# Keys and queries of a hash attention split on 128 rows for two heads and laid out by transfers, with the vector engine's constants first

## The chip, the cores and the metric

The kernel runs on one core of one Trainium2 chip. The metric is the device time of one execution in microseconds. Five engines work in order, each from its own queue: PE (TensorE, matrix products), DVE (VectorE), ACT (ScalarE), POOL (GpSimd) and SP (SyncE), which in this kernel issues every transfer.

## What is computed

An attention over hashed keys, followed by two feed-forward layers. The shapes: 2 batches, 8 heads, 768 positions, 64 numbers per head; 1536 tokens of width 512, inner width 2048.

```python
q_bits = (einsum('bhsd,dk->bhsk', q, proj) > 0)
k_bits = (einsum('bhsd,dk->bhsk', k, proj) > 0)
mask = q_bucket[:, :, :, None] == k_bucket[:, :, None, :]
scores = where(mask, scale * q @ k.T, -1e9)
attn = softmax(scores)
x = attn @ v                          # then heads side by side: 1536 x 512
x = relu(x @ w_in) ** 2 @ w_out
h = x @ moe2_w_in
out = (max(h, 0) + alpha * min(h, 0)) @ moe2_w_out
```

Six projections give each position one of 64 buckets; a query sees only the keys of its own bucket.

## The kernel before

**Stages.** The tokens are cut into four chunks of 384 queries (c = 0 to 3; chunks 0 and 1 are the first batch, 2 and 3 the second). In a chunk the 8 heads go as four pairs (j = 0 to 3), so there are 16 pairs. The attention of chunk 0 runs alone. Then the first layer of chunk c runs with the attention of chunk c + 1 spread over its steps by `Background`. After chunk 3's attention the rest is feed-forward alone.

**Precision.** A product in float32 is made of two rounded halves (high = x rounded to fp32r, low = x - high). For a score tile of head h the 128 contraction rows hold 64 rows of data and 64 more: `k1[r, h]` is the key's high half and `k1[o, h]` its low half, where `rows(h)` gives `r`, the 64 rows of the head, and `o`, the other 64. `q1` holds the query's high half on both. `k2[r, h]` repeats the key's high half and meets the query's low half `q2[r, h]`. `k2[o, h]` holds, per hash pattern, the mask of the keys (-2**100 where the pattern differs) and `q2[o, h]` the query's one-hot. So `scores` is two matrix products for each half of the keys: L317 (q1, k1) and L318 (q2, k2).

**Preparing a pair.** `load_pair` loads the keys `kr` and the queries `qn` as 128 rows (two heads below each other), and the queries a second time as `qr`, both heads side by side and the rows twice. `hash_bits` projects (L228) and compares (L232); `matches` turns signs into counts by products with the constant `code` (L244). In even chunks the keys are prepared: `k_split` (high half L254 on ACT, low half L256 on POOL, transfers L259 and L260 to the other tile or the other rows) and `k_ids` (L272). In every chunk the queries are: `q_split` (L279, L282) and `q_ids` (L291). Only pair (0, 0) makes its key halves without transfers (L262, L263).

**Order.** `attention` writes the steps of a chunk: the preparing steps of pair j + 1 stand one by one between the six score tiles of pair j, so in even chunks `q_ids` of the next pair is the last step before its first score tile; in odd chunks, which have two preparing steps, it comes four tiles earlier. The first pair of a chunk is prepared right ahead of its scores. A score tile is reduced on DVE (L321), exponentiated on ACT (L324), turned in two groups of three blocks on PE (L338), written to `pt` by ACT or DVE (L342, L344), and summed with the values (`av`, L354). The scheduler then places the instructions on the engines by its own forecast of times, so the order in a queue is not that of the text. Weights arrive as the bits of float64: `load_bits` (L459), `to_f32` (ACT L469, DVE L471, L472, L474), and store (L483); `fetch` loads converted weights again (L521). `we` and `wsg` have one buffer each.

```python
for u in range(2 * NTB):
    h, t = divmod(u, NTB)
    steps.append(lambda pr=pr, h=h, t=t: pr.scores(h, t))
    late.append((pr, h, t))
    if nxt and u > 0:
        steps.append(nxt.pop(0))
...
    if len(late) > lag:
        tail()
```

**Constants.** `constants` makes `code`, `pop` and `off`: five `iota` on POOL, then 20 short instructions on DVE (L150 to L168).

## Time and profile before

| | |
|---|---|
| runs | 858.56, 860.59, 863.87 us; median 860.59 |
| profiled execution | 862.17 us, of which span 860.2 us |
| busy in the span | PE 804.5 us (94%), DVE 515.6 (60%), ACT 487.4 (57%), POOL 385.7 (45%) |
| granted TensorE clock, mean | 0.987 |
| transfers | 118.66 MB, mean 138 GB/s |

The span runs from the first to the last instruction; 1.97 us of the profiled time lie around it. Matrix products overlap, so a busy PE is not PE at its peak: stages are to be compared by the products they hold and by the idle time that other engines' waits name.

### The profile page before, as it was taken

How to read it: one execution, taken by the hardware profiler on the slowest of the kernel's cores; microseconds unless marked ns; L12 is line 12 of the kernel's file. 1: busy time of each engine (PE TensorE's matmuls, PEld its weight loads, DVE VectorE, ACT ScalarE, POOL GpSimd, SP SyncE). 2: the span in 40 equal slices, each digit the busy share in tenths (PEclk: the TensorE clock that was granted, in tenths of full speed). 3: DMA queues.
4: the chain of work that ended last, by engine and by line, in shares of the span. 5: the costliest groups of instructions: out<-in, count | busy, mean ns of one | idle time of the engine just before them, and what ended most of it. 6: DMA issues, size and time to landing. Idle time of an engine off the chain costs nothing.

```text
span 860.2 us, 12647 instructions
## 1 busy us (share of the span) xinstructions
PE 804.5 (94%) x4384; PEld 652.2 (76%) x4384; DVE 515.6 (60%) x834; ACT 487.4 (57%) x941; POOL 385.7 (45%) x329
## 2 busy tenths in 40 slices
PE   4989899999888989999999999999999999999997
PEld 2656578776666666676867789989998998998995
DVE  5599798988577778787864431215444444444442
ACT  4768688776564655575755556654434444444341
POOL 3121133323746574562333345555555555555553
PEclk9999999999999999999999999999999999999999
DMA  6575666766666656767542388800001011001000
GB/s 193 141 229 183 196 224 228 248 213 220 181 204 206 203 182 198 213 218 222 163 142 67 88 302 299 288 1 37 3 34 38 1 38 37 1 0 37 1 1 37
DMA packets 54575, 118.66 MB, mean 138 GB/s; under 512 B 6928, under 2 KB 15344, under 8 KB 54512
## 3 DMA queue, kind: packets, MB, share of 16 engines
q1 hardware_dynamic: 54512, 117.87, 42.8%
q8 instruction: 34, 0.56, 0.3%
q14 instruction: 29, 0.24, 0.1%
HBM read 89.22 MB, written 23.12 MB: 131 GB/s over the span
## 4 chain that ended last, share of the span: by engine, by line
PE 55%; DVE 10%; DMA 6%; ACT 4%; issue 4%; POOL 2%; SPq 0%; POOLq 0%; DVEq 0%; ACTq 0%
PE acc L575 8%; PE acc L571 7%; PE acc L572 7%; PE m L545 4%; PE m L543 4%; PE m L544 4%; PE m L354 4%; PE h L543 4%; DMA w<-we 4%; PE h L544 4%; PE h L545 3%; DVE low L321 2%; PE m L338 1%; PE s L317 1%; DVE we L474 1%
## 5 line engine op out<-in xcount | busy, mean ns | idle before, releaser
L561 POOL TENSOR_TENSOR gl<-g,gh 128x384 fp32r<-128x384 f32 x128 | 136.5, 1066 | 244.8 <-ACT gh L560 123.0
L571 PE MATMUL acc<-wh,gh 128*128 128x512 f32 x384 | 160.0, 417 | 0.0
L496 POOL TENSOR_TENSOR wl<-wf,wh 128x512 fp32r<-128x512 f32 x80 | 109.4, 1370 | 112.4 <-ACT wh L495 99.9
L572 PE MATMUL acc<-wl,gh 128*128 128x512 f32 x384 | 152.6, 397 | 0.0
L495 ACT ACTIVATE wh<-w 128x512 fp32r<-128x512 f32 x128 | 80.5, 629 | 81.0 <-PE m L544 45.7
L575 PE MATMUL acc<-wh,gl 128*128 128x512 f32 x384 | 115.4, 399 | 1.8 <-POOL gl L561 1.8
L495 ACT ACTIVATE wh<-wf 128x512 fp32r<-128x512 f32 x128 | 80.4, 629 | 58.1 <-PE h L544 22.9
L543 PE MATMUL h<-xh,wh 128*128 128x384 f32 x296 | 106.4, 359 | 1.4 <-DVE pt L344 0.8
L544 PE MATMUL h<-xl,wh 128*128 128x384 f32 x296 | 100.6, 340 | 0.6 <-POOL xl L383 0.6
L545 PE MATMUL h<-xh,wl 128*128 128x384 f32 x296 | 100.8, 341 | 0.0
L321 DVE TENSOR_REDUCE low<-s 128x1 f32<-128x768 f32 x84 | 79.8, 950 | 24.9 <-PE s L318 24.3
L324 ACT ACTIVATE sm<-s,low 128x768 f32<-128x768 f32 x84 | 75.5, 899 | 30.0 <-DVE low L321 29.7
L338 PE MATMUL m<-ident,sm 128*128 128x128 f32 x525 | 84.9, 279 | 3.9 <-DVE pt L344 1.4
L575 PEld LDWEIGHTS acc<-wh,gl 128*128 128x128 f32 x384 | 72.0, 189 | 21.5 <-POOL gl L561 4.3
L496 POOL TENSOR_TENSOR wl<-w,wh 128x512 fp32r<-128x512 f32 x64 | 82.9, 1295 | 6.0 <-ACT wh L495 6.0
L571 PEld LDWEIGHTS acc<-wh,gh 128*128 128x128 f32 x384 | 72.4, 189 | 14.5 <-issue 5.0
L338 PEld LDWEIGHTS m<-ident,sm 128*128 128x128 f32 x525 | 65.9, 143 | 19.5 <-DVE pt L344 3.2
L572 PEld LDWEIGHTS acc<-wl,gh 128*128 128x128 f32 x384 | 72.8, 189 | 9.8 <-issue 1.8
L560 ACT ACTIVATE gh<-g 128x384 fp32r<-128x384 f32 x64 | 33.5, 524 | 81.5 <-DVE g L559 81.5
L317 PE MATMUL s<-k,q 128*128 128x384 f32 x168 | 64.4, 383 | 16.0 <-ACT sm L324 13.5
L558 DVE TENSOR_SCALAR r<-m,alpha_sb 128x384 f32<-128x384 f32 x43 | 26.6, 618 | 87.2 <-PE m L545 86.9
L545 PE MATMUL m<-xh,wl 128*128 128x384 f32 x216 | 73.0, 338 | 0.5 <-DVE wl L496 0.5
(107 smaller groups left out, 1536.8 us busy)
## 6 DMA issues: line engine op xcount, KB each, us to landing
wf<-w SPq DMA_DIRECT2D x96, 256.0 KB, 2.8
wbits<-in_w_in_dram SPq DMA_DIRECT2D x32, 512.0 KB, 4.1
wbits<-in_w_out_dram SPq DMA_DIRECT2D x32, 512.0 KB, 3.8
w<-wf SPq DMA_DIRECT2D x32, 256.0 KB, 3.3
w<-we SPq DMA_DIRECT2D x32, 256.0 KB, 2.1
w<-w SPq DMA_DIRECT2D x32, 256.0 KB, 4.5
qr<-in_qT_dram SPq DMA_DIRECT2D x32, 192.0 KB, 3.9
kr<-in_kT_dram SPq DMA_DIRECT2D x8, 384.0 KB
```

Of the source, the lines that this page charges most:

```text
L321: nc.vector.tensor_reduce(low, ps[:, 0:2, 0:HALF], AX.XY, ALU.max, negate=True)
L324: nc.scalar.activation(sm.rearrange("p (a n) -> p a n", a=2), ps[:, 0:2, 0:HALF], AF.Exp, bias=low, accum_out=self.sums[:, i:i + 1],)
L338: nc.tensor.transpose(ps[:, i * P:(i + 1) * P], pp[:, b * P:(b + 1) * P], ident)
L495: nc.scalar.activation(hi, w, AF.Copy)
L496: engine.tensor_tensor(lo, w, f32(hi), ALU.subtract)
L543: nc.tensor.matmul(hp, wih[:, ks], xh[:, kk, :], start=first, stop=False)
L544: nc.tensor.matmul(hp, wih[:, ks], xl[:, kk, :], start=False, stop=False)
L545: nc.tensor.matmul(hp, wil[:, ks], xh[:, kk, :], start=False, stop=last)
L561: nc.gpsimd.tensor_tensor(gl, g, f32(gh), ALU.subtract)
L571: nc.tensor.matmul(acc[:, t, :], gh[:, blocks[t]], woh, start=first, stop=False)
L572: nc.tensor.matmul(acc[:, t, :], gh[:, blocks[t]], wol, start=False, stop=False)
L575: nc.tensor.matmul(acc[:, t, :], gl[:, blocks[t]], woh, start=False, stop=last)
```

## The change

Three edits, and one that goes with them.

1. The 20 DVE instructions of `constants` and the comparisons L232 of pair (0, 0) are marked so that their written order is kept on the engine.
2. For all pairs but (0, 0) the halves are made on all 128 rows, both heads in one instruction, into tiles of their own (`kh`, `kn`, `qh`, `ql`, `qy`), and transfers put them into `k1`, `k2`, `q1`, `q2`. The low half of the keys moves from POOL to DVE. An even pair's keys take six transfers for the halves and two for the mask, where there were four; a pair's queries take four transfers from tile to tile, where there were two loads of `qr`.
3. `qr` is loaded for pair (0, 0) alone.
4. For room, `pt` has two buffers where it had three.

```diff
--- before.py
+++ after.py
@@ -90,7 +90,6 @@
     weight_pools(weights, 0)
     p1 = pool("p1", 1, att)
     p2 = pool("p2", 2, att)
-    p3 = pool("p3", 3, att)
     p4 = pool("p4", 4, att)
     sm3 = pool("sm3", 3, att)
 
@@ -134,6 +133,7 @@
 
         i32 = mybir.dt.int32
         with tc.tile_pool(name="once", bufs=1) as once:
+            first = tc.keep_in_program_order
             cols = once.tile([P, D], i32, name="cols")
             row = once.tile([P, 1], i32, name="row")
             bit = once.tile([P, 1], i32, name="bit")
@@ -147,25 +147,25 @@
             nc.gpsimd.iota(nb[:, 0, :], [[0, NB]], base=0, channel_multiplier=1)
             nc.gpsimd.iota(nb[:, 1, :], [[1, NB]], base=0, channel_multiplier=0)
 
-            nc.vector.tensor_copy(of, part)
+            first(nc.vector.tensor_copy(of, part))
             above = once.tile([P, 2 * NG], F32, name="above")
-            nc.vector.tensor_scalar(above, of, 0.0, None, ALU.is_ge)
...
-            nc.vector.tensor_scalar(sign, cols, 2.0, -1.0, ALU.mult, ALU.add)
+            first(nc.vector.tensor_scalar(above, of, 0.0, None, ALU.is_ge))
...
+            first(nc.vector.tensor_scalar(sign, cols, 2.0, -1.0, ALU.mult, ALU.add))
             for g in range(NG):
                 for h in range(2):
-                    nc.vector.tensor_scalar(
+                    first(nc.vector.tensor_scalar(
                         code[:, g, (1 - h) * D:(2 - h) * D], sign, of[:, 2 * g + h:2 * g + h + 1], None, ALU.mult
-                    )
-            nc.vector.tensor_tensor(nb[:, 0, :], nb[:, 0, :], nb[:, 1, :], ALU.logical_shift_right)
-            nc.vector.tensor_scalar(nb[:, 0, :], nb[:, 0, :], 1, None, ALU.bitwise_and)
+                    ))
+            first(nc.vector.tensor_tensor(nb[:, 0, :], nb[:, 0, :], nb[:, 1, :], ALU.logical_shift_right))
+            first(nc.vector.tensor_scalar(nb[:, 0, :], nb[:, 0, :], 1, None, ALU.bitwise_and))
             ones = once.tile([P, NB], F32, name="ones")
-            nc.vector.tensor_copy(ones, nb[:, 0, :])
...
+            first(nc.vector.tensor_reduce(pop, ones, AX.X, ALU.add))
+            first(nc.vector.tensor_scalar(off, pop, -1.0, 1.0, ALU.mult, ALU.add))
 
 
     xT = {}
@@ -186,11 +186,13 @@
                 )
         qn = p2.tile([P, T], F32, tag="qn", name="qn")
         nc.sync.dma_start(out=qn, in_=qT[b, h0:h0 + 2, :, s0:s0 + T].rearrange("h d s -> (h d) s"))
-        qr = p1.tile([P, 2, T], F32, tag="qr", name="qr")
-        for r in range(2):
-            nc.sync.dma_start(
-                out=qr[r * D:(r + 1) * D], in_=qT[b, h0:h0 + 2, :, s0:s0 + T].rearrange("h d s -> d h s")
-            )
+        qr = None
+        if c == 0 and j == 0:
+            qr = p1.tile([P, 2, T], F32, tag="kh", name="qr")
+            for r in range(2):
+                nc.sync.dma_start(
+                    out=qr[r * D:(r + 1) * D], in_=qT[b, h0:h0 + 2, :, s0:s0 + T].rearrange("h d s -> d h s")
+                )
         if c % 2 == 0:
             vr = p4.tile([P, NKB, 2 * D], F32, tag="vr", name="vr")
             nc.sync.dma_start(out=vr, in_=v[b, j])
@@ -208,6 +210,7 @@
         def __init__(self, c, j):
             self.c, self.j = c, j
             self.b = c // 2
+            self.first = c == 0 and j == 0
             self.p = {}
             self.pt = {}
 
@@ -229,7 +232,9 @@
                     ps[g * GR:(g + 1) * GR, 0:w], proj_sb.rearrange("p h n -> p (h n)"), x[:, g * w:(g + 1) * w],
                     start=True, stop=True,
                 )
-            nc.vector.tensor_scalar(bits, ps[:, 0:w], 0.0, None, ALU.is_gt)
+            ins = nc.vector.tensor_scalar(bits, ps[:, 0:w], 0.0, None, ALU.is_gt)
+            if self.first:
+                tc.keep_in_program_order(ins)
             return bits
 
         def matches(self, bits, n):
@@ -248,47 +253,75 @@
             self.k1 = p4.tile([P, 2, S], F32R, tag="k1", name="k1")
             self.k2 = p4.tile([P, 2, S], F32R, tag="k2", name="k2")
             keys[self.b, self.j][1:3] = [self.k1, self.k2]
-            shift = self.c > 0 or self.j > 0
+            if self.first:
+                for h in range(2):
+                    r, o = self.rows(h)
+                    nc.scalar.activation(self.k1[r, h], self.kr[r], AF.Copy)
+                    nc.vector.tensor_tensor(self.k1[o, h], self.kr[r], f32(self.k1[r, h]), ALU.subtract)
+                    nc.gpsimd.tensor_copy(self.k2[r, h], f32(self.k1[r, h]))
+                return
+            kh = p1.tile([P, S], F32R, tag="kh", name="kh")
+            nc.scalar.activation(kh, self.kr, AF.Copy)
+            nc.vector.tensor_tensor(self.kr.bitcast(F32R), self.kr, f32(kh), ALU.subtract)
             for h in range(2):
                 r, o = self.rows(h)
-                nc.scalar.activation(self.k1[r, h], self.kr[r], AF.Copy)
-                if shift:
-                    nc.gpsimd.tensor_tensor(
-                        self.kr[r].bitcast(F32R), self.kr[r], f32(self.k1[r, h]), ALU.subtract
-                    )
-                    nc.sync.dma_start(out=f32(self.k2[r, h]), in_=f32(self.k1[r, h]))
-                    nc.sync.dma_start(out=f32(self.k1[o, h]), in_=self.kr[r])
-                else:
-                    nc.vector.tensor_tensor(self.k1[o, h], self.kr[r], f32(self.k1[r, h]), ALU.subtract)
-                    nc.gpsimd.tensor_copy(self.k2[r, h], f32(self.k1[r, h]))
+                nc.sync.dma_start(out=f32(self.k1[r, h]), in_=f32(kh[r]))
+                nc.sync.dma_start(out=f32(self.k2[r, h]), in_=f32(kh[r]))
+                nc.sync.dma_start(out=f32(self.k1[o, h]), in_=self.kr[r])
 
         def k_bits(self):
             self.bits = self.hash_bits(self.kr, S)
 
         def k_ids(self):
             y = self.matches(self.bits, S)
+            if self.first:
+                for h in range(2):
+                    r, o = self.rows(h)
+                    nc.vector.tensor_scalar(
+                        self.k2[o, h].rearrange("p (a n) -> p a n", n=T), y[o], pop[o], NEG,
+                        ALU.not_equal, ALU.mult,
+                    )
+                return
+            kn = p1.tile([P, S], F32R, tag="kn", name="kn")
+            nc.vector.tensor_scalar(
+                kn.rearrange("p (a n) -> p a n", n=T), y, pop, NEG, ALU.not_equal, ALU.mult
+            )
             for h in range(2):
                 r, o = self.rows(h)
-                nc.vector.tensor_scalar(
-                    self.k2[o, h].rearrange("p (a n) -> p a n", n=T), y[o], pop[o], NEG, ALU.not_equal, ALU.mult
-                )
+                nc.sync.dma_start(out=f32(self.k2[o, h]), in_=f32(kn[o]))
 
         def q_split(self):
             self.q1 = p2.tile([P, 2, T], F32R, tag="q1", name="q1")
             self.q2 = p2.tile([P, 2, T], F32R, tag="q2", name="q2")
-            nc.scalar.activation(self.q1, self.qr, AF.Copy, scale=scale)
+            if self.first:
+                nc.scalar.activation(self.q1, self.qr, AF.Copy, scale=scale)
+            if self.first:
+                for h in range(2):
+                    r, o = self.rows(h)
+                    nc.vector.scalar_tensor_tensor(
+                        self.q2[r, h], self.qr[r, h], scale, f32(self.q1[r, h]), ALU.mult, ALU.subtract
+                    )
+            self.bits = self.hash_bits(self.qn, T)
+
+        def q_ids(self):
+            y = self.matches(self.bits, T)
+            if self.first:
+                for h in range(2):
+                    r, o = self.rows(h)
+                    nc.scalar.activation(self.q2[o, h], y[o, 0, :], AF.Relu, bias=off[o])
+                return
+            qh = p1.tile([P, T], F32R, tag="qh", name="qh")
+            qy = p1.tile([P, T], F32R, tag="qy", name="qy")
+            ql = p1.tile([P, T], F32R, tag="ql", name="ql")
+            nc.scalar.activation(qy, y[:, 0, :], AF.Relu, bias=off)
+            nc.scalar.activation(qh, self.qn, AF.Copy, scale=scale)
+            nc.vector.scalar_tensor_tensor(ql, self.qn, scale, f32(qh), ALU.mult, ALU.subtract)
             for h in range(2):
                 r, o = self.rows(h)
-                nc.vector.scalar_tensor_tensor(
-                    self.q2[r, h], self.qr[r, h], scale, f32(self.q1[r, h]), ALU.mult, ALU.subtract
-                )
-            self.bits = self.hash_bits(self.qn, T)
-
-        def q_ids(self):
-            y = self.matches(self.bits, T)
-            for h in range(2):
-                r, o = self.rows(h)
-                nc.scalar.activation(self.q2[o, h], y[o, 0, :], AF.Relu, bias=off[o])
+                nc.sync.dma_start(out=f32(self.q1[r, h]), in_=f32(qh[r]))
+                nc.sync.dma_start(out=f32(self.q1[o, h]), in_=f32(qh[r]))
+                nc.sync.dma_start(out=f32(self.q2[r, h]), in_=f32(ql[r]))
+                nc.sync.dma_start(out=f32(self.q2[o, h]), in_=f32(qy[o]))
 
         def prepare(self):
 
@@ -329,7 +362,7 @@
 
         def p_t(self, h, t, a):
             if t == 0 and a == 0:
-                self.pt[h] = p3.tile([P, NTB, NKB, P], F32, tag="pt", name="pt")
+                self.pt[h] = p2.tile([P, NTB, NKB, P], F32, tag="pt", name="pt")
             pp = self.p[h, t]
             ps = m_tile()
             n = NKB // 2
```

## Rows read from the trace of the kernel before

**Rows 1.** Busy time by stage: attention of chunk 0, 1 and 2.

```profile
core 0: us, PE busy (x) PEld busy (x) DVE busy (x) ACT busy (x) POOL busy (x), PEclk, DMA share, GB/s
17.20:89.20 72.00, 62.52 (x378) 44.41 (x378) 58.30 (x94) 54.37 (x113) 13.54 (x10) 0.95 0.60 182
89.20:218.00 128.80, 124.35 (x729) 92.50 (x729) 111.39 (x182) 96.60 (x196) 39.62 (x32) 0.99 0.69 223
218.00:352.00 134.00, 117.09 (x663) 89.62 (x662) 96.20 (x135) 78.49 (x155) 82.60 (x65) 0.96 0.64 197
```

**Rows 2.** Timeline of the start: start, duration, engine, line; idle before it in brackets.

```profile
5.39 2.45 DVE L262 TENSOR_TENSOR k<-kr,k 64x768 fp32r<-64x768 f32 x2
7.88 0.15 DVE L155 TENSOR_SCALAR bit<-row 128x1 int32<-128x1 int32 x1
...
9.37 0.56 DVE L282 SCALAR_TENSOR_TENSOR q<-qr,q 64x384 fp32r<-64x384 f32 x1
9.96 1.39 DVE L160 TENSOR_SCALAR code<-sign,of 128x64 bf16<-128x64 f32 x8
...
13.24 2.05 DVE L272 TENSOR_SCALAR k<-s,pop 64x768 fp32r<-64x768 f32 x2 [1.84 <-PE s L244]
...
15.22 0.24 DVE L232 TENSOR_SCALAR bits<-m 128x96 bf16<-128x96 f32 x1
...
16.48 1.18 ACT L291 ACTIVATE q<-h,off 64x384 fp32r<-64x384 f32 x2 [5.59 <-PE h L244]
...
17.20 0.66 PE L318 MATMUL acc<-k,q 128*128 128x384 f32 x1 [0.76 <-ACT q L291]
```

**Rows 3.** Timeline of two stretches in chunk 2's attention in which PE stands still.

```profile
233.57 0.69 PE L317 MATMUL s<-k,q 128*128 128x384 f32 x1 [3.70 <-ACT sm L324]
...
266.64 3.93 SPq L260 DMA_DIRECT2D k<-kr  x2
...
268.10 1.96 POOL L256 TENSOR_TENSOR kr<-kr,k 64x768 fp32r<-64x768 f32 x1
270.66 0.54 SPq L483 DMA_DIRECT2D w<-we  x1
273.89 0.66 ACT L469 ACTIVATE we<-wbits 128x512 f32<-128x512 f32 x1 [3.55 <-DMA w<-we]
275.90 0.49 PE L244 MATMUL s<-bits,code 128*128 128x192 bf16 x4 [3.37 <-ACT sm L324]
```

**Rows 4.** Busy time and granted clock around these two stretches (columns as in 1).

```profile
228.00:240.00 12.00, 8.30 (x35) 6.33 (x34) 2.56 (x4) 6.29 (x13) 5.28 (x5) 0.72 0.82 246
266.00:282.00 16.00, 12.63 (x73) 10.93 (x73) 11.52 (x15) 7.45 (x15) 11.21 (x10) 0.89 0.61 188
```

**Rows 5.** Groups by line and shape: count, then busy us and mean ns.

```profile
L256 POOL TENSOR_TENSOR kr<-kr,k 64x768 fp32r<-64x768 f32 x14 | 26.1, 1861 | 35.8 <-PE m L228 35.3
...
L279 ACT ACTIVATE q<-qr 128x768 fp32r<-128x768 f32 x16 | 13.4, 840 | 2.4 <-DMA qr<-in_qT_dram 1.8 <-PE acc L317 0.5
...
L382 ACT ACTIVATE xh<-x 128x384 fp32r<-128x384 f32 x16 | 8.3, 520 | 6.3 <-DVE x L381 6.2
```

**Rows 6.** Transfers: issue time at SP (min/median/max ns); size and us to landing.

```profile
L259 SPq DMA_DIRECT2D k<-k x14: 467/490/1142, 11.4 to 244.1; - x14
...
k<-k SPq DMA_DIRECT2D x14, 192.0 KB, 3.9
...
wf<-w SPq DMA_DIRECT2D x96, 256.0 KB, 2.8
```

**Rows 7.** Timeline of PE and ACT where a next pair's scores begin.

```profile
38.26 4.09 PE L354 MATMUL h<-pt,vr 128*64 128x384 f32 x24
...
98.37 0.44 PE L318 MATMUL s<-k,q 128*128 128x384 f32 x1 [0.36 <-ACT q L291]
...
283.79 1.17 ACT L291 ACTIVATE q<-m,off 64x384 fp32r<-64x384 f32 x2
287.70 0.34 PE L318 MATMUL s<-k,q 128*128 128x384 f32 x1
```

More of the change, by code (lines that the diff above doesn't have):

```diff
@@ L148, in constants @@
             nc.gpsimd.iota(nb[:, 1, :], [[1, NB]], base=0, channel_multiplier=0)
-            nc.vector.tensor_copy(of, part)
+            first(nc.vector.tensor_copy(of, part))
             above = once.tile([P, 2 * NG], F32, name="above")
-            nc.vector.tensor_scalar(above, of, 0.0, None, ALU.is_ge)
-            nc.vector.tensor_scalar(of, of, float(GR // 2), None, ALU.is_lt)
-            nc.vector.tensor_tensor(of, of, above, ALU.mult)
-            nc.vector.tensor_scalar(bit, row, GR // 2 - 1, None, ALU.bitwise_and)
@@ L156, in constants @@
-            nc.vector.tensor_scalar(cols, cols, bit, 1, ALU.logical_shift_right, ALU.bitwise_and)
-            nc.vector.tensor_scalar(sign, cols, 2.0, -1.0, ALU.mult, ALU.add)
+            first(nc.vector.tensor_scalar(above, of, 0.0, None, ALU.is_ge))
+            first(nc.vector.tensor_scalar(of, of, float(GR // 2), None, ALU.is_lt))
+            first(nc.vector.tensor_tensor(of, of, above, ALU.mult))
+            first(nc.vector.tensor_scalar(bit, row, GR // 2 - 1, None, ALU.bitwise_and))
+            first(nc.vector.tensor_scalar(cols, cols, bit, 1, ALU.logical_shift_right, ALU.bitwise_and))
@@ L165, in constants @@
+            first(nc.vector.tensor_tensor(nb[:, 0, :], nb[:, 0, :], nb[:, 1, :], ALU.logical_shift_right))
+            first(nc.vector.tensor_scalar(nb[:, 0, :], nb[:, 0, :], 1, None, ALU.bitwise_and))
             ones = once.tile([P, NB], F32, name="ones")
-            nc.vector.tensor_copy(ones, nb[:, 0, :])
-            nc.vector.tensor_reduce(pop, ones, AX.X, ALU.add)
-            nc.vector.tensor_scalar(off, pop, -1.0, 1.0, ALU.mult, ALU.add)
+            first(nc.vector.tensor_copy(ones, nb[:, 0, :]))
```

## Prediction

> **What bounds the kernel now.** I read three views in this order. First the busy time by stage [rows 1]: the stages that the change touches are the start, the attention of chunk 0 (17 to 89 us) and the attentions of chunks 1 to 3 beside the first layer; behind the last attention nothing of it is left. In these stages no engine is full by itself: in chunk 1's attention DVE is busy 111.39 of 128.8 us (86%) and ACT 96.60, in chunk 2's PE drops to 117.09 of 134 us and POOL rises to 82.60. Five queues work in order and wait for one another there, so time is lost where a queue's head waits, not where an engine is slow.
>
> Second, the timeline of the start [rows 2]. The first score tile can't be finished before L318 at 17.20, and the chain behind it goes through DVE: the constants begin only at 7.88, because the low halves of the keys stand ahead of them (2.45 us for both, from 5.39); `code` is made from 9.96 on; the count products can only then run, so the key mask L272 starts at 13.24 and the query's comparison L232 stands behind it at 15.22; then ACT's one-hot L291 at 16.48.
>
> Third, the two long stands of PE in chunk 2's attention [rows 3, 4]. In the second, SP holds the two moves of the keys' low halves, and the later one waits for POOL, whose subtraction from 268.10 takes 1.96 us. Behind it in SP's queue stands the store of `we`, which goes out only at 270.66; `we` has one buffer, so ACT waits 3.55 us for it, and the exponential behind ACT's conversion lets PE stand for 3.37 us. The granted clock of this stretch is 0.89, that is, part of it runs at the lower of the two levels: 0.11 x 16 = 1.8 us of full-rate work lost. The first stand costs 3.70 us, with a clock of 0.72 over 12 us: 3.4 us. It has the same shape, SP held by POOL's subtraction. Together the two cost 3.70 + 3.37 + 3.4 + 1.8 = 12.3 us.
>
> **The change part by part.**
>
> *Constants first.* They need only POOL's counting and no load, and DVE does nothing before 5 us, so the 20 instructions fit ahead: they took from 7.88 to about 11.4 with two other instructions of 0.56 us between [rows 2], so some 2.5 to 3.5 us of DVE's idle start. Costed at nothing; if the cover of 5 us were short, the comparison of the keys would be late by the difference, a few tenths. What is late next: DVE still has to do the keys' low halves (2.45), the key mask (2.05), the query's low halves (2 x 0.56) and two comparisons (0.24, and an estimate of 0.36 for the one with twice the columns), 6.2 us in all from 5.0 us on, to about 11.2; then the count products of the queries and the first L291 (half of 1.18). If the query's comparison comes last on DVE, L318 goes at about 11.2 + 0.5 + 0.6 = 12.3; if it comes early, at 9.4 to 10, behind the query's low half, which ended at 9.93. Against 17.20 that is 4.9 to 7.8 us. I take 5.0, the later end, since the order inside DVE isn't told. The bound on the other side is 0: if pair (0, 1) isn't ready when pair (0, 0)'s scores are over, the gain waits there.
>
> *ACT, DVE and POOL.* An even pair (7 of them): ACT did 2 x 0.84 for the key's high half, 0.84 for `qr` and 2 x 0.58 one-hots, 3.68 us; now 0.84 (128 rows take the time of 64 here: 64x768 took 839 ns in L254, 128x768 840 in L279) + 0.58 + 0.52 = 1.94 [rows 2, 5]; saved 1.74. DVE did 2.05 + 1.12; now 1.03 + 0.56 + the subtraction that POOL had. That one has its nearest row in L262, 2.45 / 2 = 1.2 us; saved 0.4. POOL loses 2 x 1.86 = 3.7 us [rows 5]. An odd pair (8): ACT 2.00 to 1.10, saved 0.90; DVE saves 0.56. Sum over 15 pairs: ACT 19.4, DVE 7.3, POOL 26 us. Most lies beside PE's work. In chunks 1 and 3, where only the odd pairs' saving applies, DVE is the fullest queue beside PE; 8 x 0.56 = 4.5 us is the most, 0 the least, and I take 1.0.
>
> *The held SP queue in chunk 2.* POOL's subtraction goes, DVE's takes its place at a third of the time, so the two stands [rows 3, 4] lose their cause: 12.3 us at most. But SP gets new waits of the same kind: the mask moves wait for DVE behind the count products, the query moves for ACT. The store of `we` and the loads of `wf` queue behind them, and ACT's conversion and POOL's and DVE's splits wait for those. Issues grow by 6 per even pair and 2 per odd pair, 58 in all, at 0.49 us [rows 6] 28 us of SP's time. I give back 60% of the 12.3 and take 5.0; bounds 12.3 gained and, if the new waits hold ACT as often as the old, nothing gained.
>
> *The query moves.* This is the step that can cost. Before, ACT wrote the one-hot where L318 reads it. Now four moves follow: 4 x 0.49 us of issue, 3.9 us to landing (the nearest row is the keys' half-tile move of 192 KB [rows 6]; a query move holds 96 KB, so this is the upper side), less one L291 that is saved (0.59): 5.3 us later. Who waits is PE, in order, and behind its head the layer's products. In six pairs L318 follows L291 directly (the three of chunk 0 behind the first, and the first of chunks 1, 2 and 3; 98.37 is one [rows 7]). In three pairs of chunk 2 there are 2.7 to 3.8 us between (284.96 to 287.70 is one [rows 7]). In the other six odd pairs it is over 11 us, nothing. With no cover: 6 x 5.3 + 3 x 2.6 = 39.6 us. Cover exists: beside the first layer PE has its products, and in chunk 0 the previous pair's last turns and its sum with the values, 4.09 us in one piece [rows 7], during which DVE stood idle before. The scheduler reckons with transfers when it orders PE. For chunk 0 I take 3 x 0.33 = 1.0 us lost after ACT's 1.74 per pair is counted in, with ends of 5 gained and 16 lost; for the others 0, inside the range.
>
> *The key moves* go from ACT's and DVE's work instead of ACT's and POOL's; POOL's pair took 3.7 us, so they are earlier. *`qr`* was loaded behind a wait for the buffer; that wait goes. *`pt` with two buffers*: the first eviction of a pair has to wait for the sum with the values of the pair before. In 14 of 15 handovers it did so already by the order on PE; in the first it came some 4 us ahead of the end of the block at 38.26 [rows 7]. Nothing, at most 1 us.
>
> [...] A half-tile move of 192 KB lands in 3.9 us, a whole-tile load of 256 KB in 2.8 [rows 6]. [...]
>
> **The sum.** Start -5.0, chunk 0 +1.0, chunks 1 and 3 -1.0, chunk 2 -5.0: -10.0 us. The profiled execution takes 860.2 + 1.97 = 862.17 us, so it would become 852.2; the median of the runs is 860.59, 1.6 us lower, and becomes 850.6.
>
> **The rivals.** *The moves stand at PE's head* (slower). Place: the nine pairs above. If half of the 39.6 us is uncovered, the time is 860.6 - 11.0 + 19.8 = 869.4; the gain is used up from 28% on. For it: L318 waits directly for L291 in six pairs. Against it: each wait has other PE work in reach. *SP only changes what holds it* (no change): chunk 2 gains nothing, chunk 0 loses 3 to 4 us, and the start's 5.0 us is about all: 860.6 - 5.0 - 1.0 + 3.5 = 858. For it: 28 us more of issues on the queue that caused both stands. *The start's gain is bounded elsewhere*, so that edit 1 doesn't do what it says: 860.6 - 5.0 = 856. *All held stands go*: -7.8 - 12.3 - 2 = 838.5.
>
> **How the numbers follow.** A difference under 1% (8.6 us) is about what this measurement can't tell from none: faster is below 852.0, slower above 869.2. Forecast case, 842 to 858 around 850.6: chance 0.50, of which 0.30 below 852.0 and 0.20 within. All stands go: 0.14, faster. SP changes hands or the start is bounded elsewhere: 0.18, within. Moves at PE's head: 0.18, slower. So 0.44, 0.38, 0.18. The range leaves out one in ten at each end: from 839 (the last rival) to 872 (the first, with a little over half uncovered).
>
> **What would show it.** Right: first L318 near 12 us; POOL idle in the key preparation; no store of `we` behind a move that waits for POOL; in chunk 2 a clock of 1.00. Wrong: PE or its weight loads waiting for transfers into `q` or `k` with granted clock falling after them, ACT's wait for the store of `we` above the two stands' sum, or the first scores of pair (0, 1) no earlier than before.

## The result, and the profile after

The changed kernel takes 850.87 us (median of 4 runs, 849.86 to 851.28), the kernel before 860.15 on the same chip (858.56 to 863.87). The ratio is 0.988 with an interval of 0.985 to 0.992. The forecast was 850.6 us. The profiled execution takes 850.58 us where that of before took 862.17, and its span 848.8 where it was 860.2: 11.4 us less, which is the sum to explain. By the medians it is 9.3 us: the profiled execution of before lies 2.0 us above its median, that of the changed kernel 0.3 below, and each stretch below is read from one execution.

The page of the changed kernel begins with the busy time of each engine.

```profile
PE 798.8 (94%) x4384; PEld 648.0 (76%) x4384; DVE 504.0 (59%) x819; ACT 470.5 (55%) x919; POOL 359.6 (42%) x315
```

ACT has 16.9 us less to do (forecast 19.4), DVE 11.6 (7.3), POOL 26.1 (26). The new instructions stand in the groups by line and shape; the columns are those of [rows 5].

```profile
L318 DVE SCALAR_TENSOR_TENSOR ql<-qn,qh 128x384 fp32r<-128x384 f32 x15 | 10.0, 664 | 2.9 <-DMA vr<-in_v_dram 2.3 <-ACT qh L317 0.5
L265 DVE TENSOR_TENSOR kr<-kr,kh 128x768 fp32r<-128x768 f32 x7 | 8.8, 1256 | 0.0
...
L316 ACT ACTIVATE qy<-m,off 128x384 fp32r<-128x384 f32 x14 | 8.1, 575 | 1.2 <-PE m L249 0.8 <-DMA rb<-rin 0.4
L317 ACT ACTIVATE qh<-qn 128x384 fp32r<-128x384 f32 x15 | 7.8, 521 | 0.6 <-DMA qn<-in_qT_dram 0.6
...
L264 ACT ACTIVATE kh<-kr 128x768 fp32r<-128x768 f32 x7 | 5.9, 846 | 3.1 <-DMA kr<-in_kT_dram 2.0 <-DVE kr L265 1.1
L286 DVE TENSOR_SCALAR kn<-s,pop 128x768 fp32r<-128x768 f32 x5 | 5.1, 1018 | 4.0 <-PE s L249 4.0
```

The row for POOL's subtraction [rows 5] is gone. In its place stand 7 subtractions on DVE of 1.26 us (forecast 1.2). A pair of both heads on 128 rows costs what one head on 64 rows cost: 846 ns for L264 (839 for L254 before), 1018 for the mask L286 (1016 for L272).

**The start.** The timeline of the changed kernel's start, to be held against [rows 2].

```profile
4.63 2.45 DVE L260 TENSOR_TENSOR k<-kr,k 64x768 fp32r<-64x768 f32 x2 [4.63 <-ACT k L259]
...
7.11 0.69 DVE L150 CAST of<-part 128x8 f32<-128x8 int32 x1
...
10.16 1.39 DVE L160 TENSOR_SCALAR code<-sign,of 128x64 bf16<-128x64 f32 x8
...
12.33 0.35 DVE L235 TENSOR_SCALAR bits<-m 128x192 bf16<-128x192 f32 x1
...
13.57 2.05 DVE L280 TENSOR_SCALAR k<-s,pop 64x768 fp32r<-64x768 f32 x2 [0.43 <-PE s L249]
15.54 0.24 DVE L235 TENSOR_SCALAR bits<-m 128x96 bf16<-128x96 f32 x1
...
16.81 1.18 ACT L311 ACTIVATE q<-h,off 64x384 fp32r<-64x384 f32 x2 [5.69 <-PE h L249]
...
17.53 0.66 PE L351 MATMUL acc<-k,q 128*128 128x384 f32 x1 [0.76 <-ACT q L311]
```

The constants are not DVE's first work. The keys' low halves (L260) still stand ahead of them, as in [rows 2], and `code` is made from 10.16 on, where it was 9.96. The first second product of the scores goes at 17.53 and not at the forecast 12.3; before it went at 17.20.

**The stages.** Busy time, granted clock and transfers of the changed kernel: the three stretches that answer to [rows 1], the two that answer to [rows 4], and the window of the one new stand. Then, from the timeline, this stand.

```profile
17.53:86.50 68.97, 60.77 (x378) 41.20 (x378) 45.18 (x76) 45.15 (x99) 3.03 (x3) 1.00 0.64 182
86.50:218.00 131.50, 121.95 (x699) 91.31 (x699) 113.16 (x183) 93.44 (x191) 37.84 (x31) 0.96 0.75 237
218.00:352.00 134.00, 127.84 (x760) 97.24 (x754) 91.25 (x133) 80.72 (x161) 76.98 (x64) 1.00 0.75 226
228.00:240.00 12.00, 12.00 (x68) 10.30 (x67) 6.53 (x10) 8.14 (x18) 4.75 (x5) 1.00 0.70 199
266.00:282.00 16.00, 15.15 (x95) 12.30 (x95) 10.65 (x18) 9.80 (x22) 8.72 (x9) 1.00 0.67 190
96.00:107.00 11.00, 7.55 (x22) 6.42 (x23) 6.13 (x10) 5.29 (x11) 2.01 (x2) 0.53 0.73 204
```

```profile
98.29 0.69 PE L576 MATMUL h<-xh,wh 128*128 128x384 f32 x1 [3.20 <-ACT xh L415]
```

In chunk 2's attention the clock is 1.00 throughout, and PE works 12.00 of 12 and 15.15 of 16 us where it worked 8.30 and 12.63 [rows 4]. Between 218 and 352 us PE has 760 products where it had 663 [rows 1], though the two windows don't hold quite the same work. In chunk 0 the clock is 1.00 where it was 0.95. There is one new stand, 3.20 us before 98.29, and the clock behind it is at the lower level: 0.53 over 11 us, 5.2 us of full-rate work lost. PE waits there for the high half of the layer's input from chunk 0's last pair (`xh`). The same wait, 1.41 to 3.33 us long, is in all six kernels of this document whose queries are laid out by transfers, and in the other eight it is at most 0.77 us.

To add the span up I cut both at the same work, the first product of the first layer for each chunk of tokens:

| stretch | before, us | after, us | difference | forecast |
|---|---|---|---|---|
| to the first second product of the scores | 17.2 | 17.5 | +0.3 | -5.0 |
| from there to chunk 0's layer | 72.0 | 69.0 | -3.0 | +1.0 |
| to chunk 1's layer | 152.2 | 147.7 | -4.5 | the next three together -6.0 |
| to chunk 2's layer | 148.3 | 141.2 | -7.1 | |
| to chunk 3's layer | 119.1 | 122.7 | +3.6 | |
| rest | 351.4 | 350.7 | -0.7 | 0 |

The stretch to chunk 1's layer holds the first stand of [rows 3], the one to chunk 2's the second. By the clock's records 20.4 us lay at the lower level before 510 us in the kernel before and 10.2 after. That level is 0.50, as from 233.0 to 239.5 us in the kernel before, against 1.00 elsewhere, so the difference makes 5.1 us of the 11.4. The two pages of the profile say much the same: PE is busy 5.7 us less and idle 5.7 us less.

### The profile page after: what moved, and what is told of

Same layout as the page of the kernel before. It is cut to its first block, busy times and chain, and to the rows that moved or that the text cites. A ratio compares the mean times of both kernels' runs of the same rounds, so it can differ in the third digit from the quotient of the medians.

```text
span 848.8 us, 12785 instructions
## 1 busy us (share of the span) xinstructions
PE 798.8 (94%) x4384; PEld 648.0 (76%) x4384; DVE 504.0 (59%) x819; ACT 470.5 (55%) x919; POOL 359.6 (42%) x315
## 4 chain that ended last, share of the span: by engine, by line
PE 48%; DVE 7%; DMA 3%; issue 2%; ACT 2%; POOL 1%; SPq 0%; POOLq 0%; DVEq 0%; ACTq 0%
PE acc L608 7%; PE acc L604 7%; PE acc L605 7%; PE m L578 4%; PE m L576 4%; PE m L577 4%; PE h L576 3%; PE h L577 3%; PE h L578 3%; PE m L387 3%; DMA w<-we 2%; DVE low L354 1%; DVE wsg L504 1%; DVE we L507 1%; DVE pt L377 1%
## 5 line engine op out<-in xcount | busy, mean ns | idle before, releaser
L604 PE MATMUL acc<-wh,gh 128*128 128x512 f32 x384 | 158.2, 412 | 0.0
L608 PEld LDWEIGHTS acc<-wh,gl 128*128 128x128 f32 x384 | 71.5, 188 | 21.3 <-POOL gl L594 5.0
L371 PE MATMUL m<-ident,sm 128*128 128x128 f32 x525 | 82.9, 276 | 4.0 <-ACT sm L357 1.8
L371 PEld LDWEIGHTS m<-ident,sm 128*128 128x128 f32 x525 | 64.1, 141 | 18.5 <-ACT sm L357 3.0
```

The lines of the kernel that those rows point to most:

```text
L371: nc.tensor.transpose(ps[:, i * P:(i + 1) * P], pp[:, b * P:(b + 1) * P], ident)
L604: nc.tensor.matmul(acc[:, t, :], gh[:, blocks[t]], woh, start=first, stop=False)
L608: nc.tensor.matmul(acc[:, t, :], gl[:, blocks[t]], woh, start=False, stop=last)
```

## The experiments

My theory was that of the prediction: the gain in chunk 2 comes because SP is no longer held by POOL's subtraction, and the start gives 5 us more once the constants are really first. Its rivals: the subtraction's load on POOL costs by itself, whoever waits for it; the layout by transfers and its saved ACT work are what gains; and the moved order alone does it, whatever was moved. Each kernel below is one part of the change, or the change less one part. All medians are against 859.0 to 859.3 us for the kernel before in the same series.

**`pin_all`: the constants truly first.** The changed kernel, with the key's and the query's low halves of pair (0, 0) marked as well. The mark holds an instruction behind the one that was marked before it, and does nothing against an unmarked one that is put ahead.

```diff
-                    nc.vector.tensor_tensor(self.k1[o, h], self.kr[r], f32(self.k1[r, h]), ALU.subtract)
+                    tc.keep_in_program_order(
+                        nc.vector.tensor_tensor(self.k1[o, h], self.kr[r], f32(self.k1[r, h]), ALU.subtract)
+                    )
...
-                    nc.vector.scalar_tensor_tensor(
+                    tc.keep_in_program_order(nc.vector.scalar_tensor_tensor(
                         self.q2[r, h], self.qr[r, h], scale, f32(self.q1[r, h]), ALU.mult, ALU.subtract
-                    )
+                    ))
```

> The changed kernel with the key and query low halves of pair (0, 0) on DVE pinned behind the constants too, so that the constants are really DVE's first work. Theory A (the constants were never first in the changed kernel, and the start gained nothing): here they run in DVE's idle first 5 us, the first L318-type product (second score product) moves from 17.5 to about 12.3 us and the time falls by about 5 us, to 846. Rival B (the start is absorbed, since pair (0, 1) has to be prepared anyway): the product moves, but the first layer starts no earlier than at 86.5 us and the time stays at 851 +- 2.

Measured: 845.27 us (844.71 to 848.46), ratio 0.985 (0.983 to 0.987). That is 5.6 us under the changed kernel by the medians and 2.9 by the two ratios (0.985 and 0.988 of 860), whose intervals overlap. Its timeline of the start:

```profile
1.21 0.17 DVE L150 CAST of<-part 128x8 f32<-128x8 int32 x1 [1.21 <-POOL part L146]
...
2.60 1.39 DVE L160 TENSOR_SCALAR code<-sign,of 128x64 bf16<-128x64 f32 x8
...
4.93 0.36 DVE L235 TENSOR_SCALAR bits<-m 128x192 bf16<-128x192 f32 x1
...
7.80 2.05 DVE L282 TENSOR_SCALAR k<-s,pop 64x768 fp32r<-64x768 f32 x2
9.77 1.13 DVE L303 SCALAR_TENSOR_TENSOR q<-qr,q 64x384 fp32r<-64x384 f32 x2
...
10.93 0.26 DVE L235 TENSOR_SCALAR bits<-m 128x96 bf16<-128x96 f32 x1
...
11.57 0.86 PE L231 MATMUL m<-kr,proj_sb 128*32 128x192 f32 x6
...
12.85 0.54 PE L249 MATMUL h<-bits,code 128*128 128x96 bf16 x4
...
14.15 0.66 PE L353 MATMUL acc<-k,q 128*128 128x384 f32 x1 [0.76 <-ACT q L313]
```

Now the constants run from 1.21 to 4.9 in DVE's idle start, as the prediction had it, and all on DVE is done at 11.19. The second product goes at 14.15, not at 12.3: the query's count products, ready at 11.19, stand on PE behind the next pair's projections (L231) and a first product of the scores and go at 12.85. The start gains 3.4 us on the changed kernel. Only 0.8 of it is left when chunk 0's layer begins (85.7 against 86.5); the larger part, 5.3 us, shows in the stretch to chunk 1's layer (142.4 against 147.7), where the stand at 98.29 has become one of 2.25 us at 91.16. So the constants, really first, are worth some 3 to 6 us, about what was forecast, but I can't show that all of it is the start: everything behind it is in another order.

**`no_pin`: the change without edit 1.**

```diff
-            first = tc.keep_in_program_order
+            first = lambda ins: ins
...
-            if self.first:
-                tc.keep_in_program_order(ins)
```

> The changed kernel without the marks that keep written order (edit 1 undone). Theory A (edit 1 is worth nothing): 851 +- 2, first second score product at 17.2. Rival B (the marks, by the other order that they lead to, gave the gain): 858 to 860.

Measured: 854.76 us (850.95 to 858.94), ratio 0.995 (0.993 to 0.997), 3.9 us over the changed kernel by the medians, though its second product goes at 17.0 against 17.5. It lies between the two forecasts, and its interval begins just above the changed kernel's. What edit 1 is worth here thus comes through the order that it gives to later work, not by the start.

**`pin_only`: edit 1 alone, on the kernel before**; and **`pt2_only`: `pt` with two buffers alone.**

```diff
 (pin_only)
-            nc.vector.tensor_copy(of, part)
+            first(nc.vector.tensor_copy(of, part))
...
 (pt2_only)
-                self.pt[h] = p3.tile([P, NTB, NKB, P], F32, tag="pt", name="pt")
+                self.pt[h] = p2.tile([P, NTB, NKB, P], F32, tag="pt", name="pt")
```

> The kernel before with edit 1 alone. Theory A (the constants don't come first by it, since two low halves of keys still stand ahead on DVE): 860 +- 2. Rival B (the start gains as predicted): 855.

> The kernel before with two buffers of pt instead of three, and nothing else. Forecast: 860 +- 1. It also measures how far the time moves when the scheduler merely orders the same work differently: if it lies 3 us or more from 860, differences of that size between the other kernels prove no mechanism by themselves.

Measured: 860.74 us, ratio 1.002 (1.000 to 1.004), and 859.92 us, ratio 1.000 (0.999 to 1.002). Neither does anything by itself. Yet the stretch to chunk 1's layer takes 147.2 us in the one and 150.3 in the other, against 152.2 before, and other stretches give it back. This is a measure of what reordering alone does to a stretch: several us either way. Both stands of [rows 3] are there in both (3.79 and 3.36 us, 3.86 and 3.47). In `pt2_only` the stretch to chunk 0's layer is as short as in the changed kernel, and at full clock, although POOL subtracts as before:

```profile
17.20:86.70 69.50, 59.72 (x378) 40.98 (x378) 58.26 (x93) 54.00 (x112) 13.49 (x10) 1.00 0.61 188
```

**`keys_only` and `queries_only`: the change with the queries, or with the keys, prepared as before.**

```diff
 (keys_only)
-        qr = None
-        if c == 0 and j == 0:
+        qr = p1.tile([P, 2, T], F32, tag="qr", name="qr")
...
 (queries_only)
+                if shift:
+                    nc.gpsimd.tensor_tensor(
+                        self.kr[r].bitcast(F32R), self.kr[r], f32(self.k1[r, h]), ALU.subtract
+                    )
+                    nc.sync.dma_start(out=f32(self.k2[r, h]), in_=f32(self.k1[r, h]))
+                    nc.sync.dma_start(out=f32(self.k1[o, h]), in_=self.kr[r])
```

> The changed kernel with the queries made as before (two loads of qr, halves on ACT and DVE without transfers). Theory A (the gain comes from the keys, whose low half left POOL, so that SP is no longer held): 851 +- 3, chunk 2's attention about 7 us shorter than before. Rival B (it comes from the queries, from ACT's and DVE's lighter load): 857 to 860.

> The changed kernel with the keys made as before (low half on POOL, mask written by DVE in place). Theory A (the gain comes from the keys): 858 to 862, the two stands of PE in chunk 2's attention are there in some form and the chunk takes about 148 us. Rival B (it comes from the queries): 851 to 854.

Measured: keys alone 855.14 us, ratio 0.995 (0.992 to 0.997); queries alone 859.44 us, ratio 1.000 (0.998 to 1.002). The queries' layout, most of the ACT saving with it, brings nothing alone. The keys bring 4 us; the whole change brings 9 to 10. Keys alone lie between the two forecasts, and the stretch to chunk 2's layer is 146.5 us, 1.8 shorter and not 7. Queries alone take the time that theory A gave, but without the stands: PE's longest between 86 and 510 us is 2.09 us. So POOL's subtraction can cost its time without the two long stands.

**`dve_sub`: one line of the change.** The kernel before, with the subtraction on DVE instead of POOL; halves on 64 rows, `qr`, `pt` and constants all as before. The line is written twice, one per head.

```diff
-                    nc.gpsimd.tensor_tensor(
+                    nc.vector.tensor_tensor(
                         self.kr[r].bitcast(F32R), self.kr[r], f32(self.k1[r, h]), ALU.subtract
                     )
```

> The kernel before with one engine changed: the low half of the keys (64 rows, twice per pair) on DVE instead of POOL. Theory A (SP held by POOL's subtraction makes the two long stands of PE): the stands go, chunk 2's attention falls from 148 to about 141 us, the time to 853. Rival B (the stands come from the full SP queue or from ACT's single buffer, whoever subtracts): 859 to 861.

Measured: 847.61 us (846.45 to 851.48), ratio 0.987 (0.984 to 0.990): 11.7 us less, at least as much as the whole change gives (0.988), although DVE does 14 instructions more. Its stretches to chunk 0's, 1's and 2's layer, columns as before:

```profile
17.20:86.20 69.00, 58.55 (x379) 40.90 (x379) 59.77 (x96) 53.32 (x111) 5.56 (x5) 1.00 0.57 176
86.20:230.30 144.10, 137.75 (x815) 104.03 (x816) 128.83 (x203) 109.91 (x221) 48.32 (x38) 1.00 0.71 232
230.30:375.50 145.20, 134.07 (x785) 101.97 (x784) 116.29 (x164) 89.91 (x178) 80.41 (x66) 0.99 0.65 205
```

They take 3.0, 8.1 and 3.1 us less than before. [rows 3, 4] priced the first stand at 3.70 + 3.4 = 7.1 us, which lies in the second stretch, and the second at 3.37 + 1.8 = 5.2, which lies in the third. Clock 1.00, 1.00, 0.99: both stands are gone, and a smaller one is new (2.01 us at 299.77). The three differences sum to 14.2 us, more than the 11.7 of the medians, since the traced execution of before lies 2.8 us above the median of this series. Theory A had the stands right, but not the size: the time is 5 us under its 853, and the stretch to chunk 2's layer takes 145.2 us, not 141.

In the kernel before, the first stand too goes back to SP and POOL's subtraction, but not through the store of `we`. Behind the held move SP issues a load of `kr` only at 228.02, and ACT, with the exponential behind it, waits for that load:

```profile
231.38 0.84 ACT L254 ACTIVATE k<-kr 64x768 fp32r<-64x768 f32 x1 [3.91 <-DMA kr<-in_kT_dram]
```

**`pool_sub`: the reverse.** The changed kernel with the subtraction back on POOL, on 128 rows.

```diff
-            nc.vector.tensor_tensor(self.kr.bitcast(F32R), self.kr, f32(kh), ALU.subtract)
+            nc.gpsimd.tensor_tensor(self.kr.bitcast(F32R), self.kr, f32(kh), ALU.subtract)
```

> The changed kernel with the subtraction of the keys on POOL again, now one instruction on 128 rows (about 1.85 us). Theory A (the hold of SP by POOL is the cause): half of the gain goes, 854 to 858, waits of SP for POOL's subtraction over 10 us in sum. Rival B (the layout on 128 rows gives the gain, the engine doesn't matter): 851 +- 2.

Measured: 855.44 us (853.25 to 858.17), ratio 0.995 (0.994 to 0.997). Half of the load (7 x 1.86 = 13.0 us instead of 26.1) takes 0.7% back, 4.6 us by the medians, and SP waits 12.5 us for it, both as theory A had them.

**`pool_issue`: the load without SP's wait.** The kernel before; the moves of the low halves are issued from POOL's own queue, so that SP never waits for the subtraction.

```diff
-                    nc.sync.dma_start(out=f32(self.k1[o, h]), in_=self.kr[r])
+                    nc.gpsimd.dma_start(out=f32(self.k1[o, h]), in_=self.kr[r])
```

> The kernel before, POOL still subtracting, but the two moves of the keys' low halves (L260) issued from POOL's own queue, so that SP never waits for POOL's subtraction. Theory A (SP held by that wait is what cost the time): the two stands go as with the subtraction on DVE, chunk 2's attention about 141 us, the time 848 to 852. Rival B (POOL's load, or DVE slowed beside POOL, cost the time): 857 to 860.

Measured: 857.08 us (855.19 to 859.93), ratio 0.997 (0.996 to 0.999), as rival B had it. The two stands of [rows 3] go, and others come. Two windows of it, and its timeline in three places:

```profile
228.00:252.00 24.00, 23.00 (x142) 18.19 (x141) 19.95 (x31) 18.89 (x38) 13.46 (x12) 1.00 0.72 238
...
268.00:284.00 16.00, 12.68 (x64) 10.83 (x61) 13.63 (x19) 7.93 (x15) 7.88 (x8) 0.79 0.62 192
```

```profile
219.04 0.41 PE L317 MATMUL s<-k,q 128*128 128x384 f32 x1 [3.23 <-DMA k<-kr]
...
261.61 2.19 POOL L256 TENSOR_TENSOR kr<-kr,k 64x768 fp32r<-64x768 f32 x1
...
265.39 2.54 POOL L496 TENSOR_TENSOR wl<-wf,wh 128x512 fp32r<-128x512 f32 x2
265.83 3.17 DVE L471 TENSOR_SCALAR wsg<-wbits 128x512 uint32<-128x512 uint32 x1
...
270.43 2.05 DVE L272 TENSOR_SCALAR k<-s,pop 64x768 fp32r<-64x768 f32 x2
...
272.63 0.66 PE L317 MATMUL s<-k,q 128*128 128x384 f32 x1 [3.32 <-DVE k L272]
...
273.80 0.67 ACT L469 ACTIVATE we<-wbits 128x512 f32<-128x512 f32 x1 [6.39 <-DMA w<-we]
...
301.51 7.15 DVE L474 SCALAR_TENSOR_TENSOR we<-we,wsg 128x512 uint32<-128x512 uint32 x1 [0.57 <-ACT we L469]
...
309.56 0.90 ACT L324 ACTIVATE sm<-s,low 128x768 f32<-128x768 f32 x1 [6.78 <-DVE low L321]
...
310.61 0.80 PE L244 MATMUL s<-bits,code 128*128 128x192 bf16 x4 [6.32 <-ACT sm L324]
```

The stretch to chunk 1's layer, which held the first stand, takes 144.9 us where it took 152.2: SP's wait gone, 7.3 us are gained there. The others give part of it back, 74.8 us to chunk 0's layer (72.0) and 149.5 to chunk 2's (148.3). At 219.04 PE waits 3.23 us for a move that POOL issued behind its other work. Then POOL gets to its weight splits (L496) late, DVE's conversion L471 takes 3.17 us beside them (0.56 is its mean before), the key mask comes late and PE waits 3.32 us for it; ACT waits 6.39 us for the store of `we`. At 301.51 one conversion on DVE takes 7.15 us, where the same line takes 0.69 at 274.50, while POOL does six instructions in a row beside it; the reduction of a score tile (L321) stands behind it, and PE stands for 6.32 us. Another on DVE takes 6.54 us at 216.76; in the other thirteen traces no DVE instruction takes more than 2.4 us. So the run took a wait off SP and put 14 issues of 0.55 us on POOL, and does not keep SP's wait and POOL's load apart as it was meant to.

**`dve_sub_load`: the load without any use.** DVE subtracts; POOL does as many subtractions of the same size into a tile that nobody reads (added work, nothing left out). `pt` has two buffers, for room.

```diff
+                    nc.gpsimd.tensor_tensor(junk[r], f32(self.k1[r, h]), f32(self.k1[r, h]), ALU.subtract)
                     nc.vector.tensor_tensor(
                         self.kr[r].bitcast(F32R), self.kr[r], f32(self.k1[r, h]), ALU.subtract
                     )
```

> The kernel before with the subtraction on DVE, and POOL doing a subtraction of the same size all the same, into a tile that nobody reads (64 rows x 768, both inputs the high half; for its room pt has two buffers, which by itself moved the time by nothing). SP waits for no POOL subtraction, POOL's load and its nearness to DVE are as before. Theory A (the time went with SP's wait for POOL's subtraction, and with what is queued behind it): 847 to 851. Rival B (it went with POOL's load: DVE slowed beside it, the splits of the weights behind it): 855 to 860.

Measured: 858.82 us (854.79 to 861.84), ratio 0.999 (0.998 to 1.001): all of the 11.7 us of `dve_sub` is gone. The added group, and the stretches to chunk 1's and chunk 2's layer:

```profile
L256 POOL TENSOR_TENSOR junk<-k 64x768 fp32r<-64x768 f32 x14 | 21.3, 1522 | 28.4 <-ACT k L254 28.0
```

```profile
88.00:239.00 151.00, 140.54 (x815) 104.34 (x816) 135.22 (x202) 109.00 (x219) 57.09 (x44) 0.99 0.68 220
239.00:389.40 150.40, 135.25 (x784) 102.98 (x783) 117.22 (x164) 90.39 (x179) 81.18 (x68) 0.98 0.63 201
```

Against `dve_sub` DVE is busy 135.22 instead of 128.83 us in the first stretch, with one instruction fewer and the same products on PE. Over the whole span DVE is busy 9.5 us longer with as many instructions (537.4 against 527.9 us). The load alone costs DVE time. But the added instructions don't lie where those of before lay (they run right behind L254, the first for chunk 2's keys at 118.8 us where it was 213.6), and the loss is spread from chunk 0 on (88.0, 151.0, 150.4 us against 86.2, 144.1, 145.2). `dve_sub` with two buffers of `pt` was not run; the one eviction that waits for such a buffer here waits 2.41 us, in chunk 0, and it does so in `pt2_only` too. So the run shows that such a load can cost most of the amount, not that it did so in the same places.

**`dve_sub_pin`: the line of `dve_sub` with the marks of `pin_all`**, and **`dve_sub_moves`: the line of `dve_sub` with the queries' layout by transfers, two `pt` and edit 1.**

```diff
 (both)
-                    nc.gpsimd.tensor_tensor(
+                    nc.vector.tensor_tensor(
...
 (dve_sub_pin)
+            first(nc.vector.tensor_copy(of, part))
...
+                    tc.keep_in_program_order(
+                        nc.vector.tensor_tensor(self.k1[o, h], self.kr[r], f32(self.k1[r, h]), ALU.subtract)
+                    )
...
 (dve_sub_moves)
+                nc.sync.dma_start(out=f32(self.q1[r, h]), in_=f32(qh[r]))
+                nc.sync.dma_start(out=f32(self.q1[o, h]), in_=f32(qh[r]))
+                nc.sync.dma_start(out=f32(self.q2[r, h]), in_=f32(ql[r]))
+                nc.sync.dma_start(out=f32(self.q2[o, h]), in_=f32(qy[o]))
```

> The kernel before with the subtraction on DVE, edit 1, and the low halves of pair (0, 0) pinned too, so that the constants are first; no layout by transfers. Theory A (the two gains, 11.7 us for the subtraction and 5.6 us for the constants, are apart from each other and add): 842 +- 2, below both kernels. Rival B (they share what they remove, the late start of chunk 1): 846 to 848.

> The kernel with the subtraction on DVE and keys as before, but the queries laid out by transfers, pt with two buffers and edit 1 as in the changed kernel. Theory A (the query moves cost where a pair has no slack, above all the first pair of chunk 1): 851 to 854, slower than the 847.6 with queries as before, the first second score product of chunk 1 at 100 us or later against 93.7. Rival B (they cost nothing): 846 to 848.

Measured: 845.11 us (843.4 to 848.14), ratio 0.983 (0.981 to 0.986), and 857.35 us (853.43 to 860.26), ratio 0.997 (0.995 to 0.999). With the marks the second product goes at 14.3 (17.2 in `dve_sub`), and 2.5 us are gained, within the spread of the runs and between the two forecasts. The query moves (with edit 1 and two `pt`, which did nothing on the kernel before) put 9.7 us on `dve_sub`, more than either forecast had, while in the changed kernel, put on `keys_only`, they took 4.3 off. The parts don't add up. The first second product of chunk 1 goes at 94.7 and not at 100: the loss is spread, 2.8, 4.2, 3.8 and 1.0 us in the stretches to the four layers. PE waits for the move of the one-hot twice, 1.51 us at 51.08 and 1.29 at 285.59, and 13.7 us lie at the lower clock before 510 us where `dve_sub` has 3.4, which makes 5.1 us:

```profile
51.08 0.44 PE L339 MATMUL acc<-k,q 128*128 128x384 f32 x1 [1.51 <-DMA q<-qy]
```

`dve_sub_pin` and `pin_all` are the lowest of all and can't be told apart (0.983 and 0.985; the changed kernel 0.988, with intervals that just overlap theirs).

## Why the prediction came out

The time was right to 0.3 us by luck: of the terms of the sum, two were wrong, the start by 5.3 us and chunk 0 by 4.0 the other way, and that of chunk 2 was too small.

- **Start, -5.0: wrong, +0.3.** The step that failed is "they need only POOL's counting and no load, and DVE does nothing before 5 us, so the 20 instructions fit ahead". They fit, but the mark doesn't put them there; the low halves stayed ahead, and the comparison of the keys, now held behind the constants, went from 5.00 to 12.33. The rival "the start's gain is bounded elsewhere, so that edit 1 doesn't do what it says" described this, and its 856 us would have been the time had the rest been as forecast. Where the constants are first (`pin_all`) the second product comes 3.4 us earlier, at 14.15 and not 12.3, since PE's own order puts other products before the last counts.
- **Chunk 0, +1.0: wrong in sign, -3.0.** The term counted query moves against ACT's saving. The moves hold nothing there, and the two drops of the clock in this stretch (0.95 of 72 us, 3.6 us) are gone. What did that is open. `dve_sub`, without query moves and without ACT's saving, has the same 69.0 us and a clock of 1.00, but so has `pt2_only`, in which POOL still subtracts (69.5, 1.00), while `dve_sub_moves`, in which it doesn't, takes 71.8.
- **Chunk 2, -5.0: right in place, too small.** Both stands of [rows 3] are gone, the clock is 1.00, and the stretches that hold them lost 4.5 and 7.1 us, against a most of 12.3. The 60% that I gave back for SP's new waits was not needed there: SP does wait at the lines of the new moves, 59.2 us in sum before 510 us, but only 13.6 of it falls into the stretch to chunk 2's layer, and no long stand follows from it there. The waits for POOL's splits, 50.0 us in all where there were 121.7, are not what gained: `dve_sub` keeps 121.3. But one new stand came (98.29, 3.20 us and 5.2 by the clock), and the stretch to chunk 3's layer is 3.6 us longer. `dve_sub` has neither (1.00 in its second stretch, 118.6 us to chunk 3's layer).
- **The mechanism of that term: half right.** In the kernel before both stands do follow from SP's queue, held by POOL's subtraction: the second as I read it, the first by the load of `kr`. That the subtraction on POOL costs time is shown from two sides: taking it alone off POOL gives 11.7 us, putting it back takes 4.6 away. The kernels that keep 13 us or more of such work on POOL lie at 855.4 to 860.7 us, those without at 845.1 to 857.4, so the two classes touch. That it costs through SP's wait alone is refuted by `dve_sub_load`, in which nothing waits for POOL's subtraction and 858.82 us are measured; there the load shows on DVE, which is busy 9.5 us longer than in `dve_sub` with as many instructions. `pool_issue` doesn't decide it, as it loads POOL's queue. What share the load on DVE had in before is open: the scheduler's order moves a stretch by as much as 5 us (`pin_only`, `pt2_only`). One sign speaks for a share: in each of the six kernels in which POOL makes the low halves, two or three DVE instructions take at least 1.3 us more than the quickest of their line, and in the other eight none does.
- **Query moves, cover taken for 39.6 us: held in the changed kernel.** The weight loads of L351 waited 0.4 us in all for transfers into `q`. The rival "the moves stand at PE's head" did not come there. It did, in a small way, in `dve_sub_moves`, with waits of 1.51 and 1.29 us. And the new stand at 98.29, with its clock some 8.4 us, comes only with the query moves, though PE waits for `xh` in it and not for a move; how they bring it about is not shown.
- **Chunks 1 and 3, -1.0: can't be read alone.** The stretches from 89.2 us on lost 8.0 us together, with 6.0 forecast for these and chunk 2.
- **Engines.** ACT 16.9 of 19.4 and POOL 26.1 of 26 as counted. DVE 11.6 instead of 7.3: before, DVE's instructions that ran beside POOL's subtraction took some 8 us longer in sum than the quickest fifth of their line, a term that I did not have.
- **`pt` with two buffers, nothing: right** (`pt2_only`, 1.000), though one eviction waits 2.41 us for a buffer.

One line of the change is thus worth, alone, as much as the whole. How the gain of the changed kernel divides among its parts is not shown: `pool_sub` puts 4.6 us of it on this line. The layout by transfers, which makes up most of it, saves ACT 17 us, and costs SP 58 issues; without it (`dve_sub`) the kernel is no slower.

## What to carry to other kernels

When a change has a large part and a small one, run the small one alone before writing the large: here one engine name gave a ratio of 0.987 and the whole change 0.988. A mark that keeps an order holds only among marked instructions, so read the engine's queue from the trace and mark whatever else could slip ahead. A step on an engine that is off the critical path can have two prices, who waits for it (SP, 33.2 us in all for POOL's subtraction in the kernel before) and whom it slows (DVE, 9.5 us busier in `dve_sub_load`); take away the wait alone and see whether the time goes with it, by a way that puts no new work on that engine.

## What the runs showed of the hardware

In three places a DVE instruction beside POOL took three to ten times as long as its line takes where POOL does nothing. In the kernel before, this one ran beside the subtraction of 268.10 [rows 3] (timeline):

```profile
268.39 2.22 DVE L472 SCALAR_TENSOR_TENSOR wsg<-wbits,wsg 128x512 uint32<-128x512 uint32 x1
```

It takes 0.68 us where POOL does nothing, as at 94.30 in the changed kernel (L505 there); in `pool_issue` L471 took 3.17 us beside two splits, 0.43 at 93.79 in the changed kernel (L504), and L474 took 7.15 us beside six POOL instructions in a row, 0.69 at 274.50 of the same run. By these rows the DVE instruction loses 1.5 to 6.5 us, the longest of these over more than one POOL instruction. In the kernel before, the 39 instructions of L472 that ran with POOL idle took 0.65 to 0.71 us, the 25 that ran beside it 0.65 to 2.22; what holds them there is not shown.

I had not expected that 21.3 us of work on POOL for which no instruction waits costs up to 11.2 us (`dve_sub_load` against `dve_sub`, of which the buffers of `pt` may have 2.4), on an engine that is busy 43 and 44% of the span in the two.
